# One buffer for GpSimd's squares, the query gain moved ahead of the scaling, a reordered head, and two more pairs transposed on TensorE

## The chip, the cores and the metric

The kernel runs on one core of one Trainium2 chip. The metric is device time in microseconds (us) of that core. PE is TensorE, DVE is VectorE, ACT is ScalarE, POOL is GpSimd, SP is the engine that issues most DMAs.

## The reference

Attention with RMS-normalised queries and keys, followed by a token mixer of low rank and an MLP. There are 8 batches, 12 heads, 448 tokens, head dimension 64, so the model width is 768; the MLP is 768 to 3072 to 768.

```python
def rmsnorm(x, g):
    rms = np.sqrt(np.mean(x * x, axis=-1, keepdims=True) + 1e-06)
    return x / rms * g
q_n, k_n = (rmsnorm(q, g_q), rmsnorm(k, g_k))
scores = scale * np.matmul(q_n, k_n.transpose(0, 1, 3, 2))
attn = softmax(scores)                 # written out in the reference
x = heads_joined(np.matmul(attn, v))
h = xt @ U @ V                         # xt: x with tokens last; rank 32
u = x + h.transpose(0, 2, 1)
return u + np.maximum(u @ w_ch1, 0.0) @ w_ch2
```

## The kernel before

Heads are handled in 48 pairs (six pairs to a batch) and loaded in 24 groups of four heads (t = p // 2). The order of instructions on each engine is the program's order. The first batch's attention is a head of its own; from then on the attention of batch b+1 is woven between the MLP matmuls of batch b, so that TensorE always has work.

The path of one pair: GpSimd squares q and k, VectorE sums rows, ScalarE makes 1/rms, VectorE scales (q and k times 1/rms), a transpose gives `qkT`, a gain `gg` multiplies the q half, TensorE makes the scores, ScalarE takes exponentials, TensorE multiplies by the values, and VectorE evacuates (copies out of PSUM, where the results of matmuls lie) and normalises.

```python
NE, NV, NWARM, NH = 2, 3, 16, 3
FA, FM, NPE, FA0 = 0.77, 0.09, 12, 0.5
norm = ctx.enter_context(tc.tile_pool(name="norm", bufs=2))
ps_mm = ...tile_pool(name="ps_mm", bufs=3, space=PSUM)
ps_o = ...tile_pool(name="ps_o", bufs=1, space=PSUM)

def squares(t, hs=ALL, ss=(0, 1)):
    for s in ss:                                   # s = 0: q, s = 1: k
        if (t, s) not in sqs:
            sqs[t, s] = norm.tile([SP, HG, NJ * D], FP32, tag="sq", name="sq")
        if t < 2:
            nc.scalar.activation(sqs[t, s][:, hs], qks[t][:, s, hs], AF.Square)
        else:
            nc.gpsimd.tensor_tensor(sqs[t, s][:, hs], qks[t][:, s, hs], qks[t][:, s, hs], OP.mult)

def scale(t, pr):                                  # two of these make a pair
    ...
        nc.vector.tensor_tensor(qkns[t][:, pr, s]..., qk[:, s, hp]..., rstd[:, s, hp]...to_broadcast(...), OP.mult)

def transposes(p):
    ...
    if p < NPE:                                    # on TensorE, gain while evacuating
        ... 8 x nc.tensor.transpose(...)
        nc.vector.tensor_scalar(qkT[:, 0], pt[:, 0], gg, None, OP.mult)
        nc.vector.tensor_copy(qkT[:, 1], pt[:, 1])
    else:
        nc.sync.dma_start_transpose(...qkT..., qkn)

def gains(p):
    if p >= NPE:
        nc.vector.tensor_scalar(qkTs[p][:, 0], qkTs[p][:, 0], gg, None, OP.mult)

def values(p, hh):
    ...
    if p < 6 and hh:
        o = ps_mm.tile([P, 4, D + 1], FP32, tag="mm")
    else:
        o = ps_o.tile([P, 4, D + 1], FP32, tag="o")
    ...

def attention(b, start=0):       # one pair p, woven between MLP matmuls
    ... scores(p, (0, 1)); expo(p, 0); transposes(p + 1); expo(p, 1)
        rsqrt(t + 1) if even; values(p - 1, 0)
        scale(t + 1, odd)
        scores(p, (2, 3)); expo(p, 2); values(p - 1, 1)
        squares(t + 2, ALL, (odd,)); cast_v(t + 1) if odd
        gains(p + 1)
        expo(p, 3)
        reduce(t + 2, ...)       # the row sum; pair 8 leaves its one to pair 9
        load(t + 3), load_v(t + 3) if odd
        load_w2(p - 5) if 8 <= p <= 10             # GpSimd issues this DMA
```

Of the kernel before, what the change touches and what calls it, by code (L numbers as in the profile page):

```python
# [17 lines left out]
def kernel(  # L18
# [20 lines left out]
    P = 128  # L39
# [34 lines left out]
    hT = consts.tile([P, KH, 512], BF16, name="hT")  # L74

    spare = hT.rearrange("p k n -> p (k n)").bitcast(FP32).rearrange("p (t s h e) -> p t s h e", t=2, s=3, h=HG)
    Ub = consts.tile([P, 2, 4, rank], BF16, name="Ub")
    V4 = consts.tile([P, S], BF16, name="V4")
    Vsh = consts.tile([P, 2, P], BF16, name="Vsh")
# [1 line left out]
    gk2 = consts.tile([P, 1], FP32, name="gk2")  # L81
    eps = consts.tile([SP, 1], FP32, name="eps")
    NE, NV, NWARM, NH = 2, 3, 16, 3
    FA, FM, NPE, FA0 = 0.77, 0.09, 12, 0.5
    Es = [consts.tile([SP, 2, PAD + NJ * S + PAD], BF16, name=f"E{i}") for i in range(NE)]
    vas = [consts.tile([SP, HG, NJ, D + 1], BF16, name=f"va{i}") for i in range(NV)]
    xss = [consts.tile([P, dm], BF16, name=f"xs{i}") for i in range(2)]
# [23 lines left out]
        nc.sync.dma_start(Uf, moe_U.rearrange("(p j) r -> p (j r)", j=NJ))  # L111
        nc.sync.dma_start(Vf, moe_V.rearrange("r s -> () r s").to_broadcast([4, rank, S]))

    def setup_u():
        nc.vector.tensor_copy(Uc, Uf)
        pt = ps_mm.tile([rank, S], BF16, tag="mm")
        for j in range(NJ):
            nc.tensor.transpose(pt[:, j * SP:(j + 1) * SP], Uc[:, j * rank:(j + 1) * rank], ident[:SP, :SP])
        nc.vector.tensor_copy(UT[:, PAD:PAD + S], pt)

    def setup_v():
        pt = ps_mm.tile([P, 2, 4, rank], BF16, tag="mm")
        for par in range(2):
            for i, off in enumerate(OFFS[par]):
                nc.tensor.transpose(pt[:, par, i, :], UT[:, PAD + off:PAD + off + P], ident[:rank, :rank])
        nc.vector.tensor_copy(Ub, pt)
        nc.vector.tensor_copy(V4.rearrange("r (j p) -> r j p", j=NJ), Vf.rearrange("r (p j) -> r j p", j=NJ))
        nc.vector.tensor_copy(Vsh[:, 0, 0:64], V4[:, 384:448])
        nc.vector.tensor_copy(Vsh[:, 1, 64:128], V4[:, 0:64])

    w1r = moe_w_ch1.rearrange("(o i) h -> i o h", i=P)
    w2r = moe_w_ch2.rearrange("(o i) d -> i o d", i=P)
# [24 lines left out]
    def load_v(t):  # L157
        b, h0 = t // 3, (t % 3) * HG
        if t in (2, 3):
            vt = spare[0:SP, t - 2, 2]  # L160
        else:
            vt = loads.tile([SP, HG, NJ * D], FP32, tag="vt", name="vt")
        nc.sync.dma_start(vt, v[b, h0:h0 + HG].rearrange("h (p j) d -> p h (j d)", j=NJ))
        vts[t] = vt

    def cast_v(t):
        nc.gpsimd.tensor_copy(vas[t % NV][:, :, :, 0:D], vts.pop(t).rearrange("p h (j d) -> p h j d", d=D))
# [3 lines left out]
    def squares(t, hs=ALL, ss=(0, 1)):  # L171
        for s in ss:
            if (t, s) not in sqs:
                sqs[t, s] = norm.tile([SP, HG, NJ * D], FP32, tag="sq", name="sq")
            if t < 2:
                nc.scalar.activation(sqs[t, s][:, hs], qks[t][:, s, hs], AF.Square)  # L176
            else:
                nc.gpsimd.tensor_tensor(sqs[t, s][:, hs], qks[t][:, s, hs], qks[t][:, s, hs], OP.mult)  # L178
# [8 lines left out]
    def rsqrt(t, hs=ALL):  # L187
        rs = rstds[t][:, :, hs].rearrange("p s h j -> p s (h j)")
        nc.scalar.activation(rs, rs, AF.Ln, bias=eps)
        nc.scalar.activation(rs, rs, AF.Exp, scale=-0.5)  # L190
# [44 lines left out]
    def values(p, hh):  # L235
        b = p // 6
        par = b % 2
        if b not in x3_of:
            x3_of[b] = xpool.tile([P, 3, dm], BF16, tag="x3", name="x3")
        x3, xs, E, va = x3_of[b], xss[(b // 2) % 2], Es[p % NE], vas[(p // 2) % NV]  # L240
        t0, sh, rows = (0, 3, slice(0, 64)) if par == 0 else (1, 0, slice(64, 128))
        hl = 2 * (p % 2) + hh
        d0 = (2 * (p % 6) + hh) * D
        if p < 6 and hh:
            o = ps_mm.tile([P, 4, D + 1], FP32, tag="mm")
        else:
            o = ps_o.tile([P, 4, D + 1], FP32, tag="o")
        for i, off in enumerate(OFFS[par]):
            for kc in range(NJ):
                c = PAD + kc * S + off  # L250
                nc.tensor.matmul(o[:, i, :], E[:, hh, c:c + P], va[:, hl, kc, :],  # L251
                                 start=(kc == 0), stop=(kc == NJ - 1))
        rec = attn.tile([P, 4], FP32, tag="rec")
        nc.vector.reciprocal(rec, o[:, :, D])  # L254
        nc.vector.tensor_tensor(x3[:, :, d0:d0 + D], o[:, t0:t0 + 3, 0:D],
                                rec[:, t0:t0 + 3].rearrange("p c -> p c ()").to_broadcast([P, 3, D]),
                                OP.mult)
        nc.vector.tensor_tensor(xs[rows, d0:d0 + D], o[rows, sh, 0:D],  # L258
                                rec[rows, sh:sh + 1].to_broadcast([64, D]), OP.mult)
# [101 lines left out]
    def attention(b, start=0):  # L361

        items = []

        def add(weight, fn, *args):
            items.append((weight, lambda: fn(*args)))

        for p in range(b * 6 + start, b * 6 + 6):
            t, odd = divmod(p, 2)
            add(1, scores, p, (0, 1))  # L370
            add(0, expo, p, 0)
            if p + 1 < NP:
                add(1, transposes, p + 1)
            add(1, expo, p, 1)
            if not odd and t + 1 < NT:
                add(0, rsqrt, t + 1)
            if p % 6:
                add(1, values, p - 1, 0)
            if t + 1 < NT:
                add(0, scale, t + 1, odd)  # L380
            add(1, scores, p, (2, 3))
            add(0, expo, p, 2)
            if p % 6:
                add(1, values, p - 1, 1)
            if t + 2 < NT:
                add(0, squares, t + 2, ALL, (odd,))
            if t + 1 < NT and odd:
                add(0, cast_v, t + 1)
            if p + 1 < NP:
                add(0, gains, p + 1)  # L390
            add(1, expo, p, 3)
            if t + 2 < NT and p != 8:
                add(0, reduce, t + 2, ALL, (0, 1) if p == 9 else (odd,))
            if odd and t + 3 < NT:
                add(0, load, t + 3)
                add(0, load_v, t + 3)
            if 8 <= p <= 10:
                add(0, load_w2, p - 5)
        add(1, values, b * 6 + 5, 0)
        add(1, values, b * 6 + 5, 1)  # L400
        return items

    def head():

        A, Bh = slice(0, 2), slice(2, 4)
        load(0, 2)
        load(1)
        load_v(0)
        load(2)
        load_mix()  # L410
        load_v(1)
        load_v(2)
        load(3)
        load_v(3)
        setup()
        heat(NWARM)
        squares(0, A)
        reduce(0, A)
        squares(0, Bh, (0,))
        rsqrt(0, A)  # L420
        squares(0, Bh, (1,))
        reduce(0, Bh, (0,))
        scale(0, 0)
        nc.vector.tensor_mul(gg, gg, gk2)
        transposes(0)
        reduce(0, Bh, (1,))
        rsqrt(0, Bh)
        cast_v(0)
        load_w1(0)
        load_w1(1)  # L430
        scores(0, (0, 1))
        for p in range(7):
            t, odd = divmod(p, 2)
            if p > 1:
                scores(p, (0, 1))
            expo(p, 0)
            if p > 1:
                mix_a(0, p - 2)
            if p == 0:
                scale(0, 1)  # L440
            transposes(p + 1)
            expo(p, 1)
            if p == 0:
                squares(1)
                squares(2)
            elif not odd:
                rsqrt(t + 1)
            if p:
                values(p - 1, 0)
            if p == 6:  # L450
                values(5, 1)
                mix_b(0, 4)
                mix_a(0, 5)
            elif p:
                heat(NH)
            scores(p, (2, 3))
            expo(p, 2)
            if p == 6:
                mix_b(0, 5)
            elif p:  # L460
                values(p - 1, 1)
            if 1 < p < 6:
                mix_b(0, p - 2)
            if p == 0:
                scores(1, (0, 1))
            expo(p, 3)
            if p == 0:
                reduce(1)
                rsqrt(1)
            scale(t + 1, odd)  # L470
            if p == 1:
                setup_u()
                setup_v()
            if p > 1:
                squares(t + 2, ALL, (odd,))
            reduce(t + 2, ALL, (odd,))
            if p < 2:
                load(p + 4)
                load_v(p + 4)
            if p < 6:  # L480
                heat(NH)
            if odd:
                cast_v(t + 1)
            if 0 < p < 5:
                load_w1(p + 1)

    def mixing(b):
# [69 lines left out]
```

## Time and profile before

The median is 642.47 us of 3 runs (641.62 to 643.52). Stages, read from the timeline as the start of each batch's first MLP matmul:

| stage | us |
|---|---|
| head, until the first MLP matmul | 62.6 |
| MLP of batches 0 to 7 | 72.3, 78.9, 67.8, 78.9, 70.0, 78.9, 64.7, 62.4 |
| after the last matmul | 5.0 |

Odd batches do 512 columns of matmul and even ones 384, so odd stages are longer by design. Look at the spread of the even ones (2, 4 and 6): that is where TensorE sometimes waits.

The page's busy tenths of the kernel before, in 40 slices of 16 us, show where TensorE has room:

```profile
PE   5688988999999999899999999899999999999996
...
POOL 3356043102022033202022032020223000000000
```

From the eighth slice on TensorE reads 9 but for two 8s and the last slice; before that it has room. The table of windows says the same in numbers. Its columns are window, length, busy us of PE, PEld, DVE, ACT and POOL with instruction counts, granted clock, DMA share and GB/s:

```profile
core 0: us, PE busy (x) PEld busy (x) DVE busy (x) ACT busy (x) POOL busy (x), PEclk, DMA share, GB/s
40.00:60.00 20.00, 17.59 (x226) 10.03 (x223) 17.78 (x40) 12.51 (x19) 10.25 (x10) 0.91 1.11 221
...
120.00:200.00 80.00, 80.00 (x605) 42.77 (x603) 35.98 (x82) 28.82 (x42) 13.36 (x9) 1.00 0.41 96
```

From 120 to 200 us TensorE is busy for 80.00 of 80 us: work added there costs its full length. From 40 to 60 us VectorE is as full as TensorE, and the DMA share is above 1.

What TensorE waited for in the kernel before (total us, times, longest us):

```profile
PE pt L211 <- DVE qkn L198: 7.1, 10, 1.7
PE sc L227 <- DVE qkT L219: 5.5, 6, 1.9
...
PE o L251 <- DVE xs_100 L258: 2.6, 3, 1.3
PE sc L227 <- ACT E_95 L232: 2.5, 4, 1.5
PE o L251 <- DVE xs_101 L258: 2.2, 2, 1.3
...
PE ph L333 <- DVE hT L338: 2.0, 2, 1.6
...
PE sc L227 <- ACT E_96 L232: 0.8, 2, 0.4
```

`sc <- qkT L219` is scores that wait for the gain; `o <- xs` is values that wait for the evacuation of the half before them, from the one-buffer pool; `sc <- E` is scores that wait for exponentials.

The cause behind several of these is in the timeline of the kernel before (start, length, engine, line, operation, and in brackets the idle time before it and what ended it):

```profile
94.15 1.88 POOL L178 TENSOR_TENSOR sq<-qk 112x1024 f32<-112x1024 f32 x1 [9.08 <-DMA qk<-in_q_dram]
...
95.89 4.37 DVE L198 TENSOR_TENSOR qkn<-qk,rstd 112x512 bf16<-112x512 f32 x2
...
96.82 1.91 POOL L178 TENSOR_TENSOR sq<-qk 112x1024 f32<-112x1024 f32 x1
...
98.66 1.04 POOL L167 CAST va_97<-vt 112x1024 bf16<-112x1024 f32 x1
...
100.90 0.81 PE L333 MATMUL ph<-u_371,w1b 128*128 128x384 bf16 x4 [1.62 <-DVE hT L338]
```

The two scalings of a pair start at 95.89 us and take 4.37 us together, 3.74 of them the second. They end only after both squares and a cast on GpSimd; then the relu behind them is late, and TensorE has lost 1.62 us. In the list of groups (count, then busy us and mean ns, then idle before) this is a mean of 851 ns for an operation whose median is 684:

```profile
L178 POOL TENSOR_TENSOR sq<-qk 112x1024 f32<-112x1024 f32 x40 | 75.4, 1892 | 353.6 <-DMA qk<-in_q_dram 317.9 <-DVE rec L254 16.8 <-DVE osb L352 15.2
L198 DVE TENSOR_TENSOR qkn<-qk,rstd 112x512 bf16<-112x512 f32 x88 | 71.4, 851 | 16.5 <-ACT rstd L190 16.0
```

GpSimd's squares did not give way: all 44 took 1.88 to 1.91 us. This is what the Trainium skill, "SBUF — State Buffer", section "SBUF: two separate sides", describes: the port pair that VectorE and GpSimd share is an exclusive lock, held for a whole instruction, and a VectorE operation with two SBUF inputs needs it beside a GpSimd operation that reads SBUF. The trace agrees in what is stretched: the scaling has two SBUF inputs and is stretched; row sums (one input) and evacuations from PSUM are not. It also fits that a scaling is held and not only slowed: the two longest ended about 0.55 us after GpSimd's cast did (100.25 against 99.70 us, 84.89 against 84.33). It does not show the page's order, by which the one that starts first goes first: by the profile's starts both were 0.1 to 0.3 us ahead of the square (96.51 against 96.82, 81.32 against 81.45) and yet waited for the square and the cast. Why is open.

### The profile page before, as it was taken

The page shows a single profiled execution, that of the slowest core. Times are in us where ns is not written, and L with a number is a line of the kernel's source. Part 1 is how long each engine was busy: PE and PEld are TensorE (multiplying, and loading weights), DVE is VectorE, ACT ScalarE, POOL GpSimd, SP SyncE. Part 2 cuts the span into 40 slices and gives each one's busy share as a digit, 9 for nine tenths or more (in the row PEclk, how much of TensorE's full clock was granted, in tenths as well). Part 3 has the DMA queues.
Part 4 walks back from the last instruction along what each step waited for, and adds up shares of the span by engine and source line. Part 5 has one row for each costly group of instructions (what it writes and reads, how often), then busy time and mean ns, then how long its engine had stood idle before and what let it go on. Part 6 is the DMA issues. An engine that isn't in the chain of part 4 may idle for free.

```text
span 641.5 us, 11220 instructions
## 1 busy us (share of the span) xinstructions
PE 599.3 (93%) x4741; PEld 330.7 (52%) x4741; DVE 349.7 (55%) x737; ACT 234.4 (37%) x351; POOL 122.1 (19%) x98
## 2 busy tenths in 40 slices
PE   5688988999999999899999999899999999999996
PEld 2344554544455555554555555454456555554464
DVE  4779798425646376635646366645464365342211
ACT  5357464035530454225431355205541075302100
POOL 3356043102022033202022032020223000000000
PEclk9689999999999999999999999899999999999999
DMA  9999797325346455444155355353355321040011
GB/s 202 235 245 206 165 192 153 77 67 112 76 80 158 69 115 103 125 113 115 43 113 136 79 113 116 96 120 74 79 102 151 91 39 31 26 98 2 1 50 49
DMA packets 99769, 67.66 MB, mean 105 GB/s; under 512 B 55960, under 2 KB 96136, under 8 KB 99720
## 3 DMA queue, kind: packets, MB, share of 16 engines
q1 hardware_dynamic: 91588, 57.52, 39.2%
q0 software_dynamic: 7872, 9.44, 8.7%
q8 instruction: 37, 0.61, 0.4%
q14 instruction: 12, 0.10, 0.1%
q10 hardware_dynamic: 260, 0.00, 0.0%
HBM read 52.19 MB, written 11.01 MB: 99 GB/s over the span
## 4 chain that ended last, share of the span: by engine, by line
PE 80%; DVE 13%; ACT 3%; DMA 2%; issue 1%; SPq 0%; DVEq 0%; ACTq 0%
PE po L348 33%; PE ph L333 29%; PE o L251 7%; PE sc L227 7%; DVE qkn L198 6%; DVE rstd L184 1%; DVE osb L352 1%; ACT E_95 L232 1%; PE pu L290 1%; DVE hT L338 1%; DMA qkT<-qkn 1%; DMA qk<-in_q_dram 1%; PE warm L509 1%; PE pt L211 1%; ACT E_96 L232 1%
## 5 line engine op out<-in xcount | busy, mean ns | idle before, releaser
L348 PE MATMUL po<-w2b,hT 128*128 128x384 bf16 x1344 | 235.9, 328 | 2.9 <-DVE osb L352 2.9
L348 PEld LDWEIGHTS <-hT 128*128 128x128 bf16 x1344 | 127.3, 98 | 93.6 <-issue 15.8
L333 PEld LDWEIGHTS <-w1b 128*128 128x128 bf16 x1152 | 105.9, 98 | 105.8 <-issue 16.6
L336 ACT ACTIVATE hT<-ph 128x384 bf16<-128x384 f32 (+1 forms) x96 | 52.2, 544 | 258.1 <-PE ph L333 258.1
L178 POOL TENSOR_TENSOR sq<-qk 112x1024 f32<-112x1024 f32 x40 | 75.4, 1892 | 353.6 <-DMA qk<-in_q_dram 317.9
L232 ACT ACTIVATE E_96<-sc 112x896 bf16<-112x896 f32 x96 | 85.9, 913 | 65.7 <-PE sc L227 65.7
L338 DVE TENSOR_SCALAR hT<-ph 128x384 bf16<-128x384 f32 (+1 forms) x96 | 59.7, 623 | 82.4 <-PE ph L333 81.6
L232 ACT ACTIVATE E_95<-sc 112x896 bf16<-112x896 f32 x96 | 85.8, 912 | 34.5 <-PE sc L227 34.4
L198 DVE TENSOR_TENSOR qkn<-qk,rstd 112x512 bf16<-112x512 f32 x88 | 71.4, 851 | 16.5 <-ACT rstd L190 16.0
L227 PE MATMUL sc<-qkT 64*112 64x448 bf16 x384 | 62.8, 385 | 10.6 <-DVE qkT L219 5.5
L184 DVE TENSOR_REDUCE rstd<-sq 112x16 f32<-112x1024 f32 (+1 forms) x50 | 58.2, 1167 | 6.7 <-ACT sq L176 6.6
L227 PEld LDWEIGHTS <-qkT 64*112 64x112 bf16 x384 | 21.8, 127 | 49.4 <-issue 45.1
L254 DVE RECIPROCAL rec<-o 128x4 f32<-128x4 f32 x96 | 17.2, 179 | 51.4 <-PE o L251 51.2
L251 PEld LDWEIGHTS <-E_96 112*128 112x128 bf16 x768 | 30.3, 99 | 12.5 <-DVE xs_100 L258 3.7
L251 PEld LDWEIGHTS <-E_95 112*128 112x128 bf16 x768 | 31.1, 100 | 9.4 <-issue 3.9
L333 PE MATMUL ph<-u_5051,w1b 128*128 128x512 bf16 x144 | 33.3, 379 | 0.0
L333 PE MATMUL ph<-u_3345,w1b 128*128 128x512 bf16 x144 | 33.3, 379 | 0.0
L333 PE MATMUL ph<-u_1558,w1b 128*128 128x512 bf16 x144 | 33.3, 379 | 0.0
L333 PE MATMUL ph<-u_6717,w1b 128*128 128x512 bf16 x144 | 31.2, 379 | 0.0
L333 PE MATMUL ph<-u_371,w1b 128*128 128x384 bf16 x144 | 27.0, 326 | 2.7 <-DVE hT L338 2.0
L333 PE MATMUL ph<-u_5920,w1b 128*128 128x384 bf16 x144 | 25.8, 326 | 0.0
L333 PE MATMUL ph<-u_2508,w1b 128*128 128x384 bf16 x144 | 25.6, 326 | 0.0
(110 smaller groups left out, 402.6 us busy)
## 6 DMA issues: line engine op xcount, KB each, us to landing
vt<-in_v_dram SPq DMA_DIRECT2D x22, 448.0 KB, 6.7
qk<-in_q_dram SPq DMA_DIRECT2D x21, 448.0 KB, 4.1
qk<-in_k_dram SPq DMA_DIRECT2D x21, 448.0 KB, 5.9
w1b<-in_moe_w_ch_dram POOLq DMA_DIRECT2D x6, 768.0 KB, 15.1
w2b<-in_moe_w_ch_dram POOLq DMA_DIRECT2D x6, 768.0 KB, 7.8
out_dram<-osb SPq DMA_DIRECT2D x8, 336.0 KB, 3.0
out_dram<-osb SPq DMA_DIRECT2D x8, 288.0 KB, 2.6
out_dram<-osb SPq DMA_DIRECT2D x8, 240.0 KB, 2.9
```

Source lines behind the costliest of these rows:

```text
L178: nc.gpsimd.tensor_tensor(sqs[t, s][:, hs], qks[t][:, s, hs], qks[t][:, s, hs], OP.mult)
L184: nc.vector.tensor_reduce(rstds[t][:, s, hs].rearrange("p h j -> p (h j)"), sqs[t, s][:, hs].rearrange("p h (j d) -> p (h j) d", d=D), AX, ...
L198: nc.vector.tensor_tensor(qkns[t][:, pr, s].rearrange("p j h d -> p h j d"), qk[:, s, hp].rearrange("p h (j d) -> p h j d", d=D), rstd[:, ...
L211: nc.tensor.transpose(pt.rearrange("d s (j p) -> d (s j) p", j=NJ)[:, i, :], qkn[:, i, :], ident[:SP, :SP])
L227: nc.tensor.matmul(sc[:, hh, 0:S], kT[pp, kc * SP:(kc + 1) * SP], qT[pp, :], start=True, stop=True)
L232: nc.scalar.activation(Es[p % NE][:, :, PAD + kc * S:PAD + (kc + 1) * S], scs.pop((p, kc))[:, :, 0:S], AF.Exp, scale=float(D) ** 0.5)
L251: nc.tensor.matmul(o[:, i, :], E[:, hh, c:c + P], va[:, hl, kc, :], start=(kc == 0), stop=(kc == NJ - 1))
L254: nc.vector.reciprocal(rec, o[:, :, D])
L333: nc.tensor.matmul(ph, w1b[:, dc, hc * P:(hc + 1) * P], u[:, dc, :], start=(dc == 0), stop=(dc == KD - 1))
L336: nc.scalar.activation(hT[:, hc, 0:n], ph, AF.Relu)
L338: nc.vector.tensor_relu(hT[:, hc, 0:n], ph)
L348: nc.tensor.matmul(po, hT[:, hc, i * P:(i + 1) * P], w2b[:, hc, hs], start=(hc == 0), stop=(hc == KH - 1))
```

## The change

The intent: with one buffer, a square cannot start before the row sum of the previous square is done, so GpSimd works between row sum and next scaling and not on top of a scaling. The gain moves ahead of the scaling, so that a late scaling does not hold up the scores. The first two pairs are reordered and small copies leave VectorE. Pairs 12 and 13 are transposed on TensorE. The second values of a batch's last pair use the three-buffer PSUM pool.

```diff
+    early = w2b[:, 0:11, :]...                     # room for the squares of groups 0 and 1
-    FA, FM, NPE, FA0 = 0.77, 0.09, 12, 0.5
+    FA, FM, NPE, FA0 = 0.77, 0.09, 14, 0.5
 (setup of U and V)
-        nc.vector.tensor_copy(V4..., Vf...)         # and two more copies and a cast on VectorE
+        nc.scalar.activation(V4..., Vf..., AF.Copy) # Vsh copies and the cast of U on GpSimd
 (squares)
-                sqs[t, s] = norm.tile([SP, HG, NJ * D], FP32, tag="sq", name="sq")
+                sqs[t, s] = early[0:SP, t, s] if t < 2 else norm.tile(..., tag="sq", name="sq", bufs=1)
 (values)
-        if p < 6 and hh:
+        if hh and (p < 6 or p % 6 == 5):
             o = ps_mm.tile([P, 4, D + 1], FP32, tag="mm")
 (attention)
+            if p + 1 < NP:
+                add(0, gains, p + 1)
             if t + 1 < NT:
                 add(0, scale, t + 1, odd)
 ...
-            if p + 1 < NP:
-                add(0, gains, p + 1)
 (head: pairs 0 and 1 written out)
+        expo(0, 3); reduce(1); rsqrt(1)
+        setup_v()                                   # ScalarE copies V here
+        scale(1, 0); ...
+        expo(1, 0); values(0, 0); expo(1, 1); scores(1, (2, 3)); ...
-        two groups of three warming matmuls
```

More of the change, by code (lines that the diff above doesn't have):

```diff
@@ L76 @@
     spare = hT.rearrange("p k n -> p (k n)").bitcast(FP32).rearrange("p (t s h e) -> p t s h e", t=2, s=3, h=HG)
+    early = w2b[:, 0:11, :].rearrange("p k n -> p (k n)")[:, 0:8192].bitcast(FP32).rearrange("p (t s h e) -> p t s h e", t=2, s=2, h=HG)
     Ub = consts.tile([P, 2, 4, rank], BF16, name="Ub")
@@ L112, in load_mix, with setup_u @@
         nc.sync.dma_start(Vf, moe_V.rearrange("r s -> () r s").to_broadcast([4, rank, S]))
-    def setup_u():
-        nc.vector.tensor_copy(Uc, Uf)
-        pt = ps_mm.tile([rank, S], BF16, tag="mm")
-        for j in range(NJ):
-            nc.tensor.transpose(pt[:, j * SP:(j + 1) * SP], Uc[:, j * rank:(j + 1) * rank], ident[:SP, :SP])
-        nc.vector.tensor_copy(UT[:, PAD:PAD + S], pt)
-    def setup_v():
-        pt = ps_mm.tile([P, 2, 4, rank], BF16, tag="mm")
-        for par in range(2):
-            for i, off in enumerate(OFFS[par]):
-                nc.tensor.transpose(pt[:, par, i, :], UT[:, PAD + off:PAD + off + P], ident[:rank, :rank])
-        nc.vector.tensor_copy(Ub, pt)
-        nc.vector.tensor_copy(V4.rearrange("r (j p) -> r j p", j=NJ), Vf.rearrange("r (p j) -> r j p", j=NJ))
-        nc.vector.tensor_copy(Vsh[:, 0, 0:64], V4[:, 384:448])
-        nc.vector.tensor_copy(Vsh[:, 1, 64:128], V4[:, 0:64])
+    def setup_v():
+        nc.scalar.activation(V4.rearrange("r (j p) -> r j p", j=NJ), Vf.rearrange("r (p j) -> r j p", j=NJ), AF.Copy)
+        nc.gpsimd.tensor_copy(Vsh[:, 0, 0:64], V4[:, 384:448])
+        nc.gpsimd.tensor_copy(Vsh[:, 1, 64:128], V4[:, 0:64])
+    def setup_u(step):
+        if step == 0:
+            pt = ps_mm.tile([rank, S], BF16, tag="mm")
+            for j in range(NJ):
+                nc.tensor.transpose(pt[:, j * SP:(j + 1) * SP], Uc[:, j * rank:(j + 1) * rank], ident[:SP, :SP])
+            nc.vector.tensor_copy(UT[:, PAD:PAD + S], pt)
+        else:
+            pt = ps_mm.tile([P, 2, 4, rank], BF16, tag="mm")
+            for par in range(2):
+                for i, off in enumerate(OFFS[par]):
+                    nc.tensor.transpose(pt[:, par, i, :], UT[:, PAD + off:PAD + off + P], ident[:rank, :rank])
+            nc.vector.tensor_copy(Ub, pt)
     w1r = moe_w_ch1.rearrange("(o i) h -> i o h", i=P)
@@ L173, in squares @@
             if (t, s) not in sqs:
-                sqs[t, s] = norm.tile([SP, HG, NJ * D], FP32, tag="sq", name="sq")
+                sqs[t, s] = early[0:SP, t, s] if t < 2 else norm.tile([SP, HG, NJ * D], FP32, tag="sq", name="sq", bufs=1)
             if t < 2:
@@ L427, in head @@
         rsqrt(0, Bh)
+        scores(0, (0, 1))
+        expo(0, 0)
+        scale(0, 1)
+        transposes(1)
+        expo(0, 1)
+        squares(1)
+        squares(2, ALL, (0,))
         cast_v(0)
@@ L430, in head @@
         load_w1(1)
-        scores(0, (0, 1))
-        for p in range(7):
+        nc.gpsimd.tensor_copy(Uc, Uf)
+        scores(0, (2, 3))
+        expo(0, 2)
+        scores(1, (0, 1))
+        expo(0, 3)
+        reduce(1)
+        rsqrt(1)
+        setup_v()
+        scale(1, 0)
+        reduce(2, ALL, (0,))
+        load(4)
+        load_v(4)
+        heat(NH)
+        expo(1, 0)
+        values(0, 0)
+        expo(1, 1)
+        scores(1, (2, 3))
+        expo(1, 2)
+        setup_u(0)
+        values(0, 1)
+        transposes(2)
+        expo(1, 3)
+        squares(2, ALL, (1,))
+        cast_v(1)
+        load_w1(2)
+        setup_u(1)
+        scale(1, 1)
+        reduce(2, ALL, (1,))
+        load(5)
+        load_v(5)
+        for p in range(2, 7):
             t, odd = divmod(p, 2)
-            if p > 1:
-                scores(p, (0, 1))
+            scores(p, (0, 1))
             expo(p, 0)
-            if p > 1:
-                mix_a(0, p - 2)
-            if p == 0:
-                scale(0, 1)
+            mix_a(0, p - 2)
             transposes(p + 1)
             expo(p, 1)
-            if p == 0:
-                squares(1)
-                squares(2)
-            elif not odd:
+            if not odd:
                 rsqrt(t + 1)
-            if p:
-                values(p - 1, 0)
+            values(p - 1, 0)
             if p == 6:
@@ L453, in head @@
                 mix_a(0, 5)
-            elif p:
+            else:
                 heat(NH)
@@ L459, in head @@
                 mix_b(0, 5)
-            elif p:
+            else:
                 values(p - 1, 1)
-            if 1 < p < 6:
                 mix_b(0, p - 2)
-            if p == 0:
-                scores(1, (0, 1))
             expo(p, 3)
-            if p == 0:
-                reduce(1)
-                rsqrt(1)
             scale(t + 1, odd)
-            if p == 1:
-                setup_u()
-                setup_v()
-            if p > 1:
-                squares(t + 2, ALL, (odd,))
+            squares(t + 2, ALL, (odd,))
             reduce(t + 2, ALL, (odd,))
-            if p < 2:
-                load(p + 4)
-                load_v(p + 4)
             if p < 6:
@@ L483, in head @@
                 cast_v(t + 1)
-            if 0 < p < 5:
+            if p < 5:
                 load_w1(p + 1)
```

## The prediction

> **What bounds it now.** From the first MLP matmul (62.6 us, timeline) TensorE is the limit: the table of windows has it 100% busy from 120 to 200 us, and from 120 to 641 us it idles 16.7 us in all, about 4.4 of them after the last matmul. Before 62 us VectorE leads (17.8 of 20 us in 40:60), over a DMA share near or above 1.
>
> The list of TensorE's waits and its timeline name the idle time that the change can reach:
> - scores behind the gain on q: 5.5 us, six waits, longest 1.9;
> - attention values behind the previous half's evacuation at a batch's end: 1.15 in the first, then 1.25, 1.26, 0.91 us;
> - relu or transposes behind a stretched scaling at 85.5 and 100.9 us: 1.3 and 1.6 us;
> - transposes behind scalings in the head: 7.1 us, about half from stretched ones.
>
> The cause of the stretches: a scaling (VectorE, two SBUF inputs) takes 0.68 us alone, but up to 3.74 while GpSimd squares; the pairs at 17.9, 36.1, 80.7 and 95.9 us took 3.8, 3.7, 4.2 and 4.4 us against 1.29, each ending just after GpSimd did, whose squares stay at 1.88 to 1.91. Reductions and evacuations from PSUM aren't stretched. This agrees with the Trainium skill, "GPSIMD Engine Reference", section 1 (SBUF interfaces shared, contention with VectorE instructions that have two SBUF inputs).
>
> **What the change does.**
> 1. One squares buffer: the second square waits for the first's row sum. Row sum to next scaling is 3 to 6 us, which holds a 1.89 us square and a 1.04 us cast. The first square still starts when its DMA lands, 4 to 5 us after the previous scaling; scalings are 8 to 10 us apart, so it mostly clears. Most of the 20 us excess of VectorE goes.
> 2. The gain before scaling: its transpose has landed by then (issue to landing about 3 us, the new place 5 us or more after issue). Expected: the 5.5 us disappear.
> 3. The second values at a batch's end use the other PSUM pool: 1.15 + 3.4 us disappear, less perhaps 0.3 each for that pool.
> 4. Pairs 12 and 13: sixteen more transposes, 0.57 us for eight: +1.1 us of TensorE where it has no idle time; nothing gained there.
> 5. Head: fewer warming matmuls, small copies off VectorE. ScalarE's copy of V waits for its DMA until about 21.5 us (the last V packet ends at 21.1), delaying pair 1's exponentials by 4 us; TensorE doesn't need them until values. I get pair 2's scores at about 28 instead of 30.7, then 0.5 to 2.5 us saved per stretched scaling, held near 5.3 us a pair by TensorE and by inputs (the sixth group's q lands at 55 us). First MLP matmul: about 57.
> 6. A new stall near 90 us: one pair defers its row sum, so the next does two with a square between: VectorE waits about 2 us, TensorE perhaps 1.5.
>
> **Sum.** Head -5.5; 62 to 120 us: -1.3 -1.6 -1.15 +1.8 = -2.3; later -5.5 -3.4; +1.1. That is -15.6: about 627 us. Range 619 to 634.
>
> **What would show it.** First MLP matmul near 57 us; the scaling's mean near 0.70 instead of 0.85 us, no pair over 2.5; no wait of scores on the gain; TensorE's waits for evacuations (attention values) below 1 us; DMA transposes 34 instead of 36; TensorE idle after 120 us below 9 us.
>
> **What would make it wrong.** ScalarE's early wait for V shifting the whole head; inputs arriving no earlier, so the head gains 2 us only; GpSimd's square, now chained to the row sums, landing on scalings after all; the clock staying at half longer for want of warming matmuls.
>
> Chances: faster by over 2% 0.70, within 2% 0.28, slower 0.02.

## The result

The changed kernel takes 627.24 us (median of 4, 625.73 to 627.55) against 642.39 us (4 runs) before. The ratio is 0.9758, 95% interval 0.9737 to 0.9779. Ratios here are the mean time of one kernel's fast runs over that of the other's in the same rounds, so they are not quite the ratio of the medians.

Stages of the two profiled runs (641.5 and 625.2 us), beside what the prediction expected of each:

| stage | before | after | difference | predicted |
|---|---|---|---|---|
| head | 62.58 | 56.01 | -6.6 | -5.5 |
| MLP 0 | 72.34 | 70.36 | -2.0 | -1.7 (-2.3, and half of +1.1) |
| MLP 1 | 78.90 | 79.32 | +0.4 | +0.6 (half of +1.1) |
| MLP 2, 4, 6 | 202.49 | 194.12 | -8.4 | -8.9 |
| MLP 3, 5, 7 | 220.25 | 220.28 | 0.0 | 0 |

The busy tenths after, against those of before:

```profile
PE   5698999999999999999999999999999999999996
...
POOL 2656143011211121202221033303131020000000
```

TensorE now reads 9 from the fifth slice on, three slices earlier, and the two later 8s are gone. What TensorE waited for after the change:

```profile
PE sc L230 <- ACT E_96 L235: 4.4, 4, 3.3
...
PE sc L230 <- ACT E_95 L235: 2.5, 4, 1.5
PE pt L214 <- DVE qkn L201: 2.5, 4, 1.3
PE ph L336 <- DVE hT L341: 1.9, 2, 1.1
...
PE o L254 <- DVE xs_100 L261: 0.2, 1, 0.2
PE sc L230 <- DVE qkT L222: 0.2, 1, 0.2
```

The waits of scores on the gain fell from 5.5 to 0.2 us, those of values on evacuations from 4.8 to 0.2. A wait on ScalarE has grown from 0.8 to 4.4 us; 3.3 of it is the head's wait for V, below. The groups:

```profile
L181 POOL TENSOR_TENSOR sq<-qk 112x1024 f32<-112x1024 f32 x40 | 75.7, 1893 | 363.2 <-DVE rstd L187 232.2 <-DMA qk<-in_q_dram 116.4 <-DVE rec L257 14.6
...
L201 DVE TENSOR_TENSOR qkn<-qk,rstd 112x512 bf16<-112x512 f32 x88 | 59.6, 717 | 7.1 <-ACT rstd L193 7.0
...
L222 DVE TENSOR_SCALAR qkT<-qkT,gg 128x448 bf16<-128x448 bf16 x34 | 11.9, 350 | 17.5 <-DMA qkT<-qkn 17.2
```

The scaling's mean is 717 ns. GpSimd now waits mostly for VectorE's row sums (232.2 us), which is the intended chain. The last line is new: VectorE stood idle for 17.2 us in front of the gain, waiting for DMA transposes (its waits for ScalarE's `rstd` before scalings fell from 16.0 to 7.0 us at the same time, so not all of it is added). The stretch of 4.37 us has this counterpart:

```profile
84.78 1.89 POOL L181 TENSOR_TENSOR sq<-qk 112x1024 f32<-112x1024 f32 x1 [6.64 <-DVE rstd L187]
...
86.70 1.22 DVE L187 TENSOR_REDUCE rstd<-sq 112x16 f32<-112x1024 f32 x1 [2.01 <-POOL sq L181]
...
88.44 1.91 POOL L181 TENSOR_TENSOR sq<-qk 112x1024 f32<-112x1024 f32 x1
...
89.92 1.58 DVE L201 TENSOR_TENSOR qkn<-qk,rstd 112x512 bf16<-112x512 f32 x2
...
94.71 0.97 PE L336 MATMUL ph<-u_359,w1b 128*128 128x384 bf16 x5 [1.11 <-DVE hT L341]
```

The scaling at 89.92 us takes 1.58 us. The price stands at 86.70: a row sum waits 2.01 us for the square that itself had to wait for the row sum before. The prediction had this stall as item 6.

### The profile page after: what moved, and what is told of

Read it like the earlier page. It is cut to its first block, busy times and chain, and to the rows that moved or that the text cites. A ratio compares the mean times of both kernels' runs of the same rounds, so it can differ in the third digit from the quotient of the medians.

```text
span 625.2 us, 11231 instructions
## 1 busy us (share of the span) xinstructions
PE 595.9 (95%) x4751; PEld 330.6 (53%) x4751; DVE 333.4 (53%) x735; ACT 235.6 (38%) x352; POOL 121.4 (19%) x101
## 4 chain that ended last, share of the span: by engine, by line
PE 79%; DVE 7%; DMA 6%; ACT 4%; issue 2%; POOL 1%; SPq 0%; POOLq 0%
PE po L351 33%; PE ph L336 30%; PE o L254 7%; PE sc L230 6%; DMA qkT<-qkn 2%; DMA Vf<-in_moe_V_dram 2%; DMA qk<-in_q_dram 2%; DVE qkn L201 1%; DVE osb L355 1%; DVE rstd L187 1%; ACT E_95 L235 1%; PE pu L293 1%; ACT hT L339 1%; ACT E_96 L235 1%; PE pt L214 1%
## 5 line engine op out<-in xcount | busy, mean ns | idle before, releaser
L181 POOL TENSOR_TENSOR sq<-qk 112x1024 f32<-112x1024 f32 x40 | 75.7, 1893 | 363.2 <-DVE rstd L187 232.2
L201 DVE TENSOR_TENSOR qkn<-qk,rstd 112x512 bf16<-112x512 f32 x88 | 59.6, 717 | 7.1 <-ACT rstd L193 7.0
L187 DVE TENSOR_REDUCE rstd<-sq 112x16 f32<-112x1024 f32 x44 | 53.2, 1209 | 2.4 <-POOL sq L181 2.0
```

The source lines that it names most:

```text
L187: nc.vector.tensor_reduce(rstds[t][:, s, hs].rearrange("p h j -> p (h j)"), sqs[t, s][:, hs].rearrange("p h (j d) -> p (h j) d", d=D), AX, ...
L201: nc.vector.tensor_tensor(qkns[t][:, pr, s].rearrange("p j h d -> p h j d"), qk[:, s, hp].rearrange("p h (j d) -> p h j d", d=D), rstd[:, ...
```

## The experiments

Nearly every part was undone by itself in the changed kernel, and two were done alone in the kernel before. The difference to the changed kernel is given as (ratio - 0.9758) x 642.4 us. The experiments ran in other rounds than the changed kernel, on two chips, each beside the kernel before, and each ratio has an interval of 0.0021 to 0.0035 on either side (1.3 to 2.2 us), so differences below about 2 us are not shown to be other than zero by the times alone.

| run | ratio to before | vs changed, us | first MLP matmul | MLP 0 |
|---|---|---|---|---|
| changed kernel | 0.9758 | 0 | 56.0 | 70.4 |
| two buffers again | 0.9849 | +5.8 | 58.8 | 73.6 |
| gain behind scaling again | 0.9760 | +0.1 | 55.4 | 70.3 |
| one-buffer PSUM pool again | 0.9795 | +2.4 | 55.4 | 71.3 |
| pairs 12, 13 by DMA again | 0.9841 | +5.3 | 56.2 | 76.5 |
| old head | 0.9774 | +1.0 | 55.9 | 70.9 |
| before + one buffer alone | 0.9886 | +8.2 | 56.4 | 74.9 |
| before + gain first alone | 0.9924 | +10.7 | 62.0 | 72.6 |
| V copied later | 0.9710 | -3.1 | 50.3 | 70.7 |
| pairs by DMA, weights early | 0.9765 | +0.4 | 55.3 | 70.7 |
| V later, row sum split | 0.9775 | +1.1 | 53.3 | 74.4 |
| all of these, pairs by DMA | 0.9767 | +0.6 | 52.6 | 74.2 |
| before + squares on ScalarE | 0.9966 | +13.4 | 58.4 | 73.5 |

### Two buffers again

```diff
-... norm.tile([SP, HG, NJ * D], FP32, tag="sq", name="sq", bufs=1)
+... norm.tile([SP, HG, NJ * D], FP32, tag="sq", name="sq")
```

> The changed kernel with two buffers for the squares again (gain still ahead of the scaling). Theory 1, GpSimd's squares on top of scalings are what cost: stretched scalings come back (mean from 0.72 to 0.80 us or more, some pairs over 3 us), first MLP matmul 1 to 3 us later, and the total is 3 to 6 us above the changed kernel's 627.2 us. Theory 2, the order of gain and scaling is what counted and the single buffer did little: at most 1 us slower, even if scalings are stretched.

It took 633.3 us. The longest scaling is 3.74 us again, the head is 2.8 us longer and the first MLP 3.2 us longer. MLP 2, 4 and 6 stay as fast as in the changed kernel (65.1, 64.5, 63.8 us). So theory 1 holds, but the single buffer earns its time in the first 130 us; later, the gain's new place covers for stretched scalings.

### The gain behind the scaling again

```diff
-            if p + 1 < NP:                 # ahead of scale
-                add(0, gains, p + 1)
             add(0, scale, t + 1, odd) ... add(0, cast_v, t + 1)
+            if p + 1 < NP:                 # behind cast_v
+                add(0, gains, p + 1)
```

> The changed kernel with the gain put back behind the scaling (one buffer stays). The prediction gave 5.5 us to the gain's place, so by its sum this run is 5.5 us slower than the changed kernel, with waits of scores on the gain of about 5 us. Rival: four of those six waits (5.0 of 5.5 us) stood behind stretched scalings, which the single buffer removes by itself; then this run is 0 to 1 us slower, waits of scores on the gain below 1 us, and VectorE's new waits for the DMA transposes are gone.

It took 627.85 us, no slower than the changed kernel within the interval. Scores waited for the gain on DMA-transposed pairs this little (list of TensorE's waits):

```profile
PE sc L230 <- DVE qkT L222: 0.8, 2, 0.4
```

The rival holds. With the single buffer in place, the gain's place is worth nothing that the times show. VectorE's waits for DMA transposes are gone too, and the mean scaling is 692 ns (717 in the changed kernel).

### The gain first, alone, and the single buffer, alone

The first puts the gain ahead of the scaling in the kernel before; the second gives the kernel before one buffer (with the separate room for groups 0 and 1).

```diff
 (gain first alone: the same two lines moved ahead of scale in the kernel before)
 (one buffer alone)
+    early = w2b[:, 0:11, :]...
-                sqs[t, s] = norm.tile(..., tag="sq", name="sq")
+                sqs[t, s] = early[0:SP, t, s] if t < 2 else norm.tile(..., tag="sq", name="sq", bufs=1)
```

> The kernel before with the gain ahead of the scaling, nothing else. If the gain's place is worth its waits even with stretched scalings: 4 to 5.5 us faster. If a stretched scaling delays the next transposes and relus just as much: 0 to 3 us faster, and the 4 us pair of scalings at 80 and 96 us stays.

> The kernel before with the single buffer for squares (and the separate place for the first two groups' squares), nothing else. If stretched scalings also caused the waits on the gain: 8 to 11 us faster than before, waits of scores on the gain below 1 us. If the gain's place is a separate term of 5.5 us: 3 to 5 us faster, with the waits on the gain still about 5 us.

The gain alone made the kernel 4.9 us faster ((1 - 0.9924) x 642.4), although scalings were still stretched up to 3.99 us; MLP 2 and 4 became 1.0 and 3.9 us shorter. The single buffer alone made it 7.3 us faster: head -6.2 us, MLP 2 and 4 -1.7 and -3.9 us, but MLP 0 +2.6 us. Both parts remove most of the 5.5 us of waits on the gain, which all lay in MLP 2 and 4, so either suffices there, and their gains do not add. With the single buffer alone the line of 5.5 us reads:

```profile
PE sc L228 <- DVE qkT L220: 1.2, 5, 0.4
```

The gain first, alone, leaves 1.2 us too. The expectation of 8 to 11 us for the single buffer was just missed, by the profiles because of the longer MLP 0. There VectorE waited 2.0 us, until 101.6 us, for the transpose of pair 12 (issued at 92.3), and TensorE waited 1.15 us at 99.6 and 3.11 us at 104.4 us for evacuations. The next pair of runs shows this wait at its largest, and its cause.

### Pairs 12 and 13 by DMA again, and then with the weights out of the way

```diff
-    FA, FM, NPE, FA0 = 0.77, 0.09, 14, 0.5
+    FA, FM, NPE, FA0 = 0.77, 0.09, 12, 0.5
```

> The changed kernel with pairs 12 and 13 transposed by DMA again. Theory 1: sixteen transposes less on a TensorE without idle time, 0.7 to 1.3 us faster than the changed kernel, no new wait. Rival: their transposes stand in the sync queue behind loads and stores, scores wait for them, and the run is 0 to 3 us slower.

It took 633.23 us, 5.3 us more than the changed kernel by the ratios: the opposite of theory 1, and more than the rival gave. The timeline of this run:

```profile
90.49 0.81 POOL L142 DMA_DIRECT2D w2b<-in_moe_w_ch_dram  x1
...
91.79 1.45 SPq L218 DMA_TRANSPOSE qkT<-qkn  x1
...
101.01 0.34 DVE L222 TENSOR_SCALAR qkT<-qkT,gg 128x448 bf16<-128x448 bf16 x1 [4.95 <-DMA qkT<-qkn]
...
103.46 1.06 PE L254 MATMUL o<-va,E 112*128 112x65 bf16 x16 [5.45 <-DVE xs L261]
```

GpSimd issues the last load of the second weight at 90.49 us. The transpose of pair 12 is issued at 91.79 and lands at 101.0 (9.2 us; the median is 3.5). VectorE, in order, stands 4.95 us in front of the gain, and TensorE 5.45 us for the evacuation behind it. The transpose's first packet ran at 95.7 us. In the packet records between 94 and 98 us, 478 packets of the weights (1,536 bytes) ran and only 171 of the transpose's 896 packets (256 bytes); 619 of them ran between 98 and 100 us, when the weights ended.

To tell weights from other loads, the next run issues the last three weight loads early and changes nothing else:

```diff
     head()
-        for i in range(3):
+        for i in range(6):
             load_w2(i)
 ...
-            if 8 <= p <= 10:
-                add(0, load_w2, p - 5)
```

> The changed kernel with pairs 12 and 13 by DMA again (as in the run that was 6.0 us slower), and the last three loads of the second weight issued with the first three at 55 us, not between squares. Theory 1: pair 12's transpose was late (9.2 us, landed at 100.9) because its packets ran behind those weight loads, and VectorE stood at the gain: now it lands within 4 us, TensorE's 5.5 us wait goes, and the total is 0 to 1.5 us below the changed kernel's 627.2 us. Rival: q, k and v loads or the sync queue delay it: the 5 us wait stays, and the run is still 4 us or more above the changed kernel.

It took 626.84 us. The transpose of pair 12, issued at nearly the same time, landed after 3.2 us (at 93.7 us), and the gain did not wait:

```profile
90.53 1.51 SPq L218 DMA_TRANSPOSE qkT<-qkn  x1
...
95.81 0.34 DVE L222 TENSOR_SCALAR qkT<-qkT,gg 128x448 bf16<-128x448 bf16 x1
...
95.83 0.69 PE L254 MATMUL o<-va,E 112*128 112x65 bf16 x16
```

So the weights were the cause. This also says why the kernel before did not suffer: there the transpose was issued at 100.33 us, as the last weight load (issued at 96.00, landed at 103.0) was ending, and landed 3.7 us later. The run with the single buffer alone, where the last load was issued at 90.98 and the transpose at 92.28 us, had the same late landing (9.3 us), so the single buffer is what brings them together. In the changed kernel it puts GpSimd's weight loads behind squares that wait for row sums (the middle one of the three issued at 87.6 instead of 84.3 us) while the shorter head brings the transpose forward to about 91 us. The two meet. Two more pairs on TensorE avoid the meeting.

### The one-buffer PSUM pool again

```diff
-        if hh and (p < 6 or p % 6 == 5):
+        if p < 6 and hh:
```

> The changed kernel with the second values of a batch's last pair back in the one-buffer PSUM pool. Theory 1: TensorE again waits about 1.2 us for the evacuation at the end of batches 1, 3, 5, 7, so 3.5 to 4.6 us slower. Rival: the wait moves to another place in the weave and the time changes by less than 1.5 us.

It took 629.56 us, +2.4 us by the ratios (the intervals of the two ratios, 0.977 to 0.982 and 0.9737 to 0.9779, overlap slightly). In the profiled run the wait is back in full:

```profile
PE o L254 <- DVE xs L261: 4.5, 5, 1.4
```

MLP 0, 2, 4 and 6 are 0.9, 0.7, 0.8 and 0.9 us longer than in the changed kernel, 3.2 us together before rounding. Theory 1 holds in mechanism; the time found is 2.4 to 3.2 us and not the 4.5 us of the waits.

### The old head

```diff
 def head():
-    (pairs 0 and 1 written out, setup of U and V on ScalarE and GpSimd)
+    (the head of the kernel before, with its warming matmuls and its setup of U and V on VectorE)
```

> The changed kernel with the old head (order of pairs 0 and 1, warming matmuls and the setup of U and V as before), all else changed. Theory 1: the reordering is worth about 2 us of the head's 6.6 us and the single buffer the rest: first MLP matmul at 57.5 to 59 us, total 1.5 to 3 us above the changed kernel. Rival: the reordering is worth nothing, as ScalarE's wait for V (4.5 us) costs what the shorter order gains: within 1 us of the changed kernel.

It took 628.39 us (+1.0 us, inside the intervals), and its first MLP matmul started at 55.9 us, as early as in the changed kernel. The rival holds: on top of the single buffer the reordering as it stands adds nothing. It seems not empty by itself: with two buffers, the new head reached its first MLP matmul at 58.8 us, against 62.6 before (that run also has the gain first, which alone gave 62.0, and the separate room for the first squares, which no run tried by itself). The two parts remove partly the same time, and the single buffer with its separate room is enough for it.

### V copied later

The changed kernel's timeline names what the reordering lost:

```profile
22.32 0.99 ACT L116 ACTIVATE V_90<-Vf 128x448 bf16<-128x448 f32 x1 [4.47 <-DMA Vf<-in_moe_V_dram]
...
23.21 3.33 ACT L235 ACTIVATE E_96<-sc 112x896 bf16<-112x896 f32 x4
...
24.16 0.62 PE L230 MATMUL sc<-qkT 64*112 64x448 bf16 x2 [3.34 <-ACT E_96 L235]
```

ScalarE waits 4.47 us for V to arrive, and the exponentials of pair 1 and TensorE's next scores (3.34 us) wait behind it. V is not needed there.

```diff
         rsqrt(1)
-        setup_v()
 ...
         expo(1, 3)
         squares(2, ALL, (1,))
+        setup_v()
```

> The changed kernel with the copy of V moved behind pair 1's exponentials. ScalarE then does not wait for V before pair 1; TensorE's 3.3 us wait at 20.8 us before pair 1's second scores falls to about 0.3 us. Theory 1: the head shortens by 1 to 3 us (first MLP matmul at 53 to 55 us) and the total by the same. Rival: loads hold the head (the second half of group 2 and V arrive no earlier), gain below 0.5 us.

It took 623.9 us, ratio 0.971 (0.9685 to 0.9736) and the fastest of all kernels here. Pair 1's exponentials start at 17.91 us instead of 23.21, and TensorE's scores at 20.41 instead of 24.16:

```profile
17.91 1.71 ACT L235 ACTIVATE E<-sc 112x896 bf16<-112x896 f32 x2
...
20.41 0.99 PE L230 MATMUL sc<-qkT 64*112 64x448 bf16 x4
...
22.68 1.01 ACT L116 ACTIVATE V<-Vf 128x448 bf16<-128x448 f32 x1
```

TensorE's waits for exponentials fell from 6.9 us (4.4 and 2.5) to 3.9. The profiled run's first MLP matmul started at 50.3 us. The next two kernels have the same head and started at 53.3 and 52.6 us, so the head itself varies by some 3 us from run to run. Still, these three lie apart from the five profiled runs with the changed kernel's head and single buffer, which started between 55.3 and 56.2 us: a move of some 2 us at the least stands out of the spread.

Another thing moved with it. The mean granted clock of TensorE between 20 and 40 us was 0.66 in the changed kernel and 0.96, 0.83 and 0.88 in these three, highest where the MLP began first. No run separates what the missing wait is worth from what the higher clock is worth; the clock is not all, since the run with the old head had 0.90 there and began its MLP at 55.9 us.

### V later and the row sum of pair 8 in its own pair, and with everything

```diff
-            if t + 2 < NT and p != 8:
-                add(0, reduce, t + 2, ALL, (0, 1) if p == 9 else (odd,))
+            if t + 2 < NT:
+                add(0, reduce, t + 2, ALL, (odd,))
 (the second run adds the early weights and NPE = 12)
```

> The changed kernel with the copy of V moved behind pair 1's exponentials, and the deferred row sum of pair 8 put back in its own pair. Theory: the 2.0 us wait of VectorE between the two row sums near 85 us goes, and with it 1.0 to 2.1 us of TensorE's waits in the first MLP: 1 to 2 us below the run with V moved alone (623.9 us). Rival: group 6's q then lands too late for the earlier row sum (the head is shorter), VectorE waits for GpSimd as long: no gain, or up to 1 us worse.

> As the run before, with the weight loads early and pairs 12 and 13 by DMA. If early weights only remove the collision: 0.5 to 1.5 us faster than the run before (sixteen transposes less on TensorE). If they delay group 6's inputs: slower by up to 3 us.

They took 627.07 and 626.93 us: neither beats V moved alone. The deferred row sum was there for a reason:

```profile
74.89 1.89 POOL L181 TENSOR_TENSOR sq<-qk 112x1024 f32<-112x1024 f32 x1 [15.74 <-DMA qk<-in_q_dram]
...
76.82 1.22 DVE L187 TENSOR_REDUCE rstd<-sq 112x16 f32<-112x1024 f32 x1 [2.48 <-POOL sq L181]
...
78.68 1.14 PE L336 MATMUL ph<-u,w1b 128*128 128x384 bf16 x6 [1.47 <-DVE hT L341]
```

Group 6's q lands at about 74.9 us, so a row sum in pair 8 stands 2.48 us in front of its square (and another 3.17 us near 92 us), and MLP 0 grows to 74.4 us. The rival of the expectation holds. Of the 6.1 us between the profiled runs of the row-sum kernel and of V moved alone (628.7 against 622.6 us), about 3 are the later start of the first MLP, with the same code up to there, and 3.6 the longer MLP 0; the other stages give a little back.

### Squares on ScalarE

This takes GpSimd's squares away from the kernel before and leaves both buffers and all orders as they were.

```diff
-            if t < 2:
+            if t < NT:
                 nc.scalar.activation(sqs[t, s][:, hs], qks[t][:, s, hs], AF.Square)
```

> The kernel before with all squares on ScalarE, two buffers kept, nothing else changed: GpSimd then runs only casts. Theory 1: scalings take 1.3 us a pair throughout (mean below 0.72 us), waits of scores on the gain fall below 1 us, total 4 to 9 us faster than before, unless ScalarE's 40 more microseconds delay exponentials in the head. If stretched scalings stay over 2 us a pair, the cause is not GpSimd's squares.

Every scaling is now short (the view of one tile's instructions: count, then shortest, median and longest ns):

```profile
L198 DVE TENSOR_TENSOR qkn<-qk,rstd x88: 672/682/693, 8.8 to 533.7; 112x512 bf16<-112x512 f32 x88
...
L198 DVE TENSOR_TENSOR qkn<-hT,rstd x8: 672/674/943, 36.1 to 52.6; 112x512 bf16<-112x512 f32 x8
```

That settles the cause of the stretches: none of the 88 scalings is over 0.70 us, and of the eight from the spare room the longest is 0.94. TensorE's waits changed to these:

```profile
PE sc L227 <- ACT E L232: 11.4, 12, 5.1
...
PE sc L227 <- DVE qkT L219: 1.7, 3, 0.9
```

The waits of scores on the gain fell from 5.5 to 1.7 us with the order unchanged, though not below the 1 us expected. The time improved by only 2.2 us ((1 - 0.9966) x 642.4), below the 4 to 9 expected: TensorE now waits 11.4 us for exponentials, against 3.3 us (2.5 and 0.8) in the kernel before, which goes a long way to explain the rest. ScalarE is the wrong home for the squares.

## Why the prediction was right or wrong

The time (627.0 predicted, 627.2 measured) and the ledger by stages were right, the first within its range and every stage within about 1 us. Of the parts behind that ledger, some were not as stated. That the total agreed to 0.2 us is partly luck: the new schedule brings a collision worth 5.3 us, and the two pairs on TensorE avoid it, and neither was foreseen; the PSUM term was too large and the head's too small. Two of the signs named beforehand were missed narrowly: scores still waited 0.2 us on the gain, and TensorE idled 9.8 us after 120 us, not below 9 (17.2 before, by the table of windows).

- **Stretched scalings, single buffer (right).** The mean went from 851 to 717 ns (0.70 predicted), no pair is over 2.39 us. The squares-on-ScalarE run shows the cause without a change of order. The stall of 2 us near 90 us came as foreseen.
- **"The gain before scaling ... the 5.5 us disappear" (right as an observation, wrong as a term).** The waits went, but four of the six stood behind stretched scalings (5.0 of 5.5 us), and the single buffer removes those by itself: the gain put back costs 0.1 us. The sum counted the 5.5 us only once, so the total did not suffer.
- **"Its transpose has landed by then" (wrong).** VectorE waited 17.2 us in front of the gain, eleven times, up to 3.7 us. TensorE had enough queued for this to cost 0.2 us of waits on the gain. The median of 3.5 us from issue to landing hid a tail of 8.5 us that was in the trace before.
- **"Pairs 12 and 13: ... nothing gained there" (wrong).** The cost of eight transposes is 0.4 us in MLP 1, near the 0.57 predicted. But without them the kernel is 5.3 us slower, because the other parts of the change bring the DMA transpose of pair 12 into the weight loads. The prediction looked for a wait in the trace before, where the two do not meet.
- **Second PSUM pool (mechanism right, size too large).** Undoing it costs 2.4 us by the ratios and 3.2 by the stages, not 4.5.
- **Head (size near, split wrong).** The first MLP matmul came at 56.0 (57 predicted), and ScalarE's wait for V was there (until 22.3 us, 21.5 predicted). The clock did stay low for longer, as the prediction feared (0.50 from 20 to 30 us, 0.66 before). But the prediction gave the reordering 2.7 of the 5.5 us, and the old-head run shows that it adds nothing on top of the single buffer, which alone moves the first MLP matmul to 56.4 us. The parts of the head were added up in the sum although they overlap: with two buffers, the new head (with the gain first and the separate room) still gave 3.8 us.

What stays open: the run-to-run variation of the head (3 us among three runs with the same head), how much of V's gain is the wait and how much the higher clock, and what the separate room for the first squares is worth without the single buffer.

## What to carry to other kernels

When two engines share a resource, look for the same operation taking several lengths and ask what the other engine did at that moment; of the ways tried here by themselves, one buffer fewer was worth most (7.3 us; the gain's place 4.9, squares on ScalarE 2.2). Parts of a change that cure one wait can't be added up, and a part that looks like pure cost in the old trace may be what keeps the new schedule from a collision: undo each part in the new kernel before judging it. An in-order engine should not be given an early instruction whose input comes from a DMA, unless the input is known to be there.

## What the Trainium skill lacked or had wrong

- "SBUF — State Buffer", sections "SBUF: two separate sides" and "Summary: rules for kernel authors", names the contention and the rule that the second to issue blocks. The runs agree in part: a GpSimd cast that takes 1.04 us elsewhere took 1.50 us beside a scaling that stood before it (at 400.42 us in the trace of the kernel before). But the two longest scalings, 3.57 and 3.74 us, began 0.1 to 0.3 us before the square that they then waited for, so who came first in the profile did not decide there (starts on GpSimd are rough). What the page lacks, beyond advice to schedule the one that is off the critical path, is a way to keep the two apart in a kernel whose order is fixed by tiles: here one buffer fewer was worth 5.8 us when undone and 7.3 us alone.
- "DMA: Bandwidth & Descriptors", section "Queues, rings and completion order", has each DMA engine take turns between queues packet by packet. It gives no figure for what that does to a transpose beside a bulk load: here landing took 9.2 us behind a weight load and 3.2 us without it, its first packet ran 3.9 us after the issue (1.3 without the weights), and most of its packets (619 of 896) ran in the 2 us in which the weights ended. The records of packets do not show turns one for one (478 of the weights against 171 of the transpose between 94 and 98 us); no run here shows how the turns are dealt.
